# One tile and one write per block for the softmax weights p, loads without the own segment and partly from ScalarE's queue, q products a step later

## Chip, cores and metric

One core of a Trainium2 chip runs the whole program. The metric is the device time of one execution in microseconds (us). All arrays are float32; matmuls run in a float32 form for which every operand is split in two parts (below).

## What is computed

```python
xn = _layernorm(x)                        # x: 2048 x 512
q  = (xn @ wq)                            # 32 heads of 128
p  = softmax(q @ k.T * 128**-0.5)         # per head, the last 512 cached keys
o  = p @ v                                # per head, back to 128 columns
s  = concat(o) @ wo                       # 4096 -> 512
z  = gelu(xn @ w_in)                      # 688 + 688 columns
g  = w_sp @ layernorm(z[:, 688:]) + b_sp  # 2048 x 2048 times 2048 x 688
out = x + s * silu((z[:, :688] * g) @ w_out)
```

The first five lines are the attention part, to which the change belongs; it fills the span up to about 1535 us. The rest follows it.

## The kernel before, in words

**Two parts of every operand.** A value is kept as `hi` (rounded by ScalarE) and `lo` (the rest, from VectorE or GpSimd by `rest`, L59). A product is three matmuls, hi·hi, hi·lo and lo·hi (`mm3`, L65 to L67).

**Blocks and steps.** A block is one head with 512 rows of q; there are 128 blocks, and each has four steps of 128 rows, 512 steps `t` in all. One loop over `t` writes out the order of all engines by hand: each stage stands a fixed number of steps ahead of or behind the scores. In step `t`:

- `score(t)` (L468): q·k into a PSUM tile `ps_3` (ring of 4), the row maximum on VectorE (`nm`, L475), the exponential on ScalarE (`prob`, L477).
- `turn(t-1)` (L479): VectorE transposes the 32x32 squares of `prob` (L486) into a tile, SyncE (SP) writes that to HBM (`p_dram`, L491), and after a block's fourth step VectorE takes the reciprocal of the row sums (L493).
- `turned(b)` (L495), in step 4b+7: the turned p comes back from HBM into `pL` with the partition groups exchanged, so that keys stand on the partitions.
- `shares(b, c)` (L501), 11 steps after the score: ScalarE casts a quarter of p to `pT_h` (L506), GpSimd makes `pT_l`.
- `pv(b, c)` (L510), 13 steps after: p·v, summed in a PSUM tile `ps_a` (a pool of 4 banks); after the fourth one `pv_out` makes `oT_h` on ScalarE (L521) and `oT_l` on VectorE.
- `outp(b, j)` (L526), 18 steps after: o·wo into a `ps_3`, added to `sacc` on VectorE (L536).

**q.** From the second group of four blocks on, q is made by a scheme with seven products for two heads and two halves of the columns: `q_products` (L439 to L448) runs in the 16 steps that begin LEAD steps before the group's first score, `q_evict` (L451) and `q_done` take the results out. A group holds up to three `ps_a` banks; the one called `a` is read last by the eviction with index 6: `qT_h` on ScalarE (L378), then `qT_l` on VectorE. That `qT_l` is put on the list `late` and runs at a step's end, so the profile gives it the line of the loop over that list, L728.

**Queues.** Each engine works through its own instructions in order, SP and ScalarE their transfers too. Before, SP issues all transfers of the attention part: weights (`raw`, L102; `wq`, L409), p out and back, and stored parts of x (`rawx` to `x_dram`, L314; the fetches of L258 and L263). ScalarE issues only the stores of z1 (L358). Eight semaphores are shared by all transfers of both queues in turn, so a transfer can also wait for an earlier one that used its semaphore.

Of the kernel before, what the change touches and what calls it, by code (L numbers as in the profile page):

```python
# [8 lines left out]
F32 = mybir.dt.float32  # L9
# [8 lines left out]
P = 128  # L18
# [14 lines left out]

XL, QL, ML, PL, OL = 11, 7, 11, 13, 18
T8 = NT // 2
LEAD = 13
Q = 32


# [1 line left out]
def mixer_kernel(ctx: ExitStack, tc: tile.TileContext, x, wh, w_in, w_sp, b_sp, w_out, out):  # L41
# [8 lines left out]
    nc = tc.nc  # L50
# [3 lines left out]
    dram = ctx.enter_context(tc.tile_pool(name="dram", bufs=1, space=DRAM))  # L54
# [3 lines left out]
    def rest(engine, lo, whole, hi):  # L58
        engine.tensor_tensor(lo, whole, hi.bitcast(F32), op=OP.subtract)  # L59

    late = []
# [23 lines left out]
    att = ExitStack()  # L85
    sp = att.enter_context(tc.tile_pool(name="sp", bufs=1))
    ap = att.enter_context(tc.tile_pool(name="ap", bufs=2))
    wq = att.enter_context(tc.tile_pool(name="wq", bufs=2))
    zs = att.enter_context(tc.tile_pool(name="zs", bufs=2))
    xq = att.enter_context(tc.tile_pool(name="xq", bufs=4))  # L90
    sacc = sp.tile([P, T8, D], F32, name="sacc")


# [3 lines left out]
    raw, wt = {}, {}  # L97
# [5 lines left out]

    def load_early(n, cs):
        if (n, "raw") not in raw:
            raw[n, "raw"] = ap.tile([P, 16, P], F32, name="pL").rearrange("p k q -> p (k q)")
        for lo, hi in cs:
            nc.sync.dma_start(raw[n, "raw"][:, lo * NB:hi * NB].rearrange("p (c f) -> p c f", f=NB), w_in[n, :, lo:hi])
            for k in range(lo, hi):
                raw[("w", n), k] = raw[n, "raw"][:, k * NB:k * NB + NB]  # L110
# [237 lines left out]
    def z1_product(i, n, between=lambda: None):  # L348
        ps = ps_acc.tile([P, 512], F32, name="ps_a") if n else ps_step.tile([P, 512], F32, name="ps_3")
        zmm(ps[:, :NB], i, n, range(2))  # L350
        between()
        zmm(ps[:, :NB], i, n, range(2, NC))
        return ps
# [7 lines left out]
        z1_out(i, n, z1_product(i, n, between))  # L361


    pB = [None]
    qps, qT, pps, pD, pL, pT, oT, prob, sums = {}, {}, {}, {}, {}, {}, {}, {}, {}

    def where(b):
# [21 lines left out]
    def qproj(b, c):  # L389
        h, qb = where(b)  # L390
        if c == 0:
            qps[b] = ps_acc.tile([P, 512], F32, name="ps_a")
        mm3(qps[b], c == 0, c == NC - 1, cols(wt[("q", h), 0], c * P, (c + 1) * P),
            tuple(X[0][c // 2, qb][:, a, c % 2] for a in range(2)))
# [56 lines left out]
    def q_evict(g, k):  # L451
        ps = qps[g, BANK[k]]
        if k in (0, 2, 3):
            t = qps[g, "t", k] = ap.tile([P, 512], F32, name="qs", bufs=2)
            nc.scalar.activation(t, ps, AF.Copy, scale=SCALE)  # L455
        elif k in (1, 5):
            nc.vector.scalar_tensor_tensor(ps, ps, SCALE, qps[g, "t", {1: 0, 5: 2}[k]], op0=OP.mult, op1=OP.add)
        elif k == 4:
            t = qps[g, "t", 3]
            nc.vector.scalar_tensor_tensor(t, ps, SCALE, t, op0=OP.mult, op1=OP.add)  # L460
# [18 lines left out]
    def turn(t):  # L479

        b, j = divmod(t, 4)
        if j % 2 == 0:
            pB[0] = ap.tile([P, 4, 2, P], F32, name="pB", bufs=3)
        nc.vector.transpose(pB[0][:, :, j % 2, :].rearrange("p a (c q) -> p a c q", q=Q),  # L486
                            prob.pop(t).rearrange("p (a c q) -> p a c q", a=4, q=Q))
        if j == 0:
            pD[b] = dram.tile([2, P, 1024], F32, name="p_dram", bufs=3)
        if j % 2:  # L490
            nc.sync.dma_start(pD[b][j // 2], pB[0].rearrange("p a j f -> p (a j f)"))  # L491
        if j == 3:
            nc.vector.reciprocal(sums[b], sums[b])  # L493

    def turned(b):  # L495
        pL[b] = ap.tile([P, 8, 256], F32, name="pL")
        of = pD.pop(b).rearrange("s (i r) (a f) -> a r (s i) f", i=4, a=4)
        for a in range(4):
            nc.sync.dma_start(pL[b][Q * a:Q * a + Q], of[a])

    def shares(b, c):  # L501
        hi = ap.tile([P, 512], F32R, name="pT_h", bufs=4)
        lo = ap.tile([P, 512], F32R, name="pT_l", bufs=4)
        p = pL[b].rearrange("p i (j f) -> p (i j) f", j=2)[:, :, Q * c:Q * c + Q]
        h, l = (t.rearrange("p (i q) -> p i q", q=Q) for t in (hi, lo))
        nc.scalar.copy(h, p)  # L506
        rest(nc.vector if 4 * b + c >= NSTEP - 10 and c % 2 else nc.gpsimd, l, p, h)
        pT[b, c] = (hi, lo)
# [6 lines left out]
    def pv_out(b, c):  # L515
        if c == 3:
            hi = ap.tile([P, 512], F32R, name="oT_h")
            lo = ap.tile([P, 512], F32R, name="oT_l")
            ps = pps.pop(b).rearrange("p (s i j q) -> p s i j q", s=2, i=4, j=2)
            h, l = (t.rearrange("p (s j i q) -> p s i j q", s=2, i=4, j=2) for t in (hi, lo))  # L520
            nc.scalar.copy(h, ps)  # L521
            for k in range(2):
                late.append((rest, nc.vector, l[:, k], ps[:, k], h[:, k]))
            oT[b] = (hi, lo)

    def outp(b, j):  # L526
# [44 lines left out]
    for g in range(1, NG):  # L571
        t0 = 16 * g - LEAD
        loads.setdefault(max(T0, t0 - 12), []).append(g)
        sums_at, splits_at = (-5, -4, -2, 1), (-3, -1, 2, 4, 6, 7, 10)
        if g == 1:
            sums_at, splits_at = (-5, -4, 1, 3), (0, 1, 3, 5, 6, 8, 10)
        order = sorted([(s, 1, q_sum, k) for k, s in enumerate(sums_at)] + [(s, 0, q_split, k) for k, s in enumerate(splits_at)])
        for s, _, f, k in order:
            at(t0 + s, f, g, k)
        for k in range(7):  # L580
            done = next(s for s in range(16) if 6 * k + 5 in q_span(g, s))
            q_events.setdefault(t0 + done, []).append((q_evict, g, k))
            if k in (1, 4, 5):
                q_events.setdefault(t0 + done + 1, []).append((q_done, g, k))
            elif k == 6:
                q_events.setdefault(t0 + done + 2, []).append((q_done, g, k))
# [7 lines left out]
    for k, d in enumerate((4, 6, 8, 11, 13, 15, 17)):  # L594
        for n in range(4):
            ends.setdefault(16 * (NG // 2 - 1) - LEAD + d + (0, 0, 1, 1)[n], []).append((fetch_part, 1, ORDER[k], n))
    ends.setdefault(16 * (NG - 1) - LEAD + 9, []).append((fetch_x, 1, (0, 1)))
    for k in ((0, 0), (1, 0)):
        ends.setdefault(NSTEP + 6, []).append((fetch_x, 0, k))
    n = 0  # L600
    for p in range(4):
        seq, store = later_x(p)
        for f, ks in seq:
            t = 30 + 13 * n // 5
# [5 lines left out]

    load_x(0, 1)
    load_early(0, [(0, 2)])
    load_x(1, 2)
    load_early(0, [(2, 4)])
    load_x(2, 4)
    load_early(1, [(0, 4)])
    load_piece(("q", 0), 0)
    load_x(4, 8)
# [27 lines left out]
    ps = ps_step.tile([P, 512], F32, name="ps_3")  # L646
# [9 lines left out]
    ps = ps_step.tile([P, 512], F32, name="ps_3")  # L656
# [4 lines left out]
    ps = ps_acc.tile([P, 512], F32, name="ps_a")  # L661
# [18 lines left out]
    for t in range(T0, T1):  # L680
# [9 lines left out]
        i = t + XL  # L690
        if i < T8:
            ln_flip(i)
        if 0 <= bm < NBLK:
            shares(bm, cm)
# [8 lines left out]
        if 0 <= bq < 4:  # L703
            qproj(bq, cq)
        g, s = divmod(t + LEAD, 16)
        if 0 < g < NG:
# [5 lines left out]
        if t in DRAIN:  # L712
            ps = z1_product(*DRAIN[t])
# [19 lines left out]
    ps = z1_product(*LAST[-1])  # L733
# [276 lines left out]
```

## Time and profile before

| | us |
|---|---|
| median of 3 runs | 1907.47 |
| lowest, highest | 1906.44, 1908.14 |
| profiled execution, its own time | 1907.01 |
| span of its profile | 1905.1 |

PE is TensorE's matmul, PEld its weight load, DVE is VectorE, ACT ScalarE, POOL GpSimd; an SPq or ACTq row is an instruction in that queue. A row of waits reads: who waited, at which line, for whom, then us in total, times, and the longest. A row of a table by stages has the busy us of the five engines with their counts of instructions, the granted TensorE clock, the share of time in which the 16 DMA engines were busy, and what they moved in GB/s. A group of instructions shows its count, busy us in all, ns of one, and the idle us of its engine just before it with what ended them. In a timeline stand start, length, and in brackets the idle time before.

### The profile page before, as it was taken

The page shows a single profiled execution, that of the slowest core. Times are in us where ns is not written, and L with a number is a line of the kernel's source. Part 1 is how long each engine was busy: PE and PEld are TensorE (multiplying, and loading weights), DVE is VectorE, ACT ScalarE, POOL GpSimd, SP SyncE. Part 2 cuts the span into 40 slices and gives each one's busy share as a digit, 9 for nine tenths or more (in the row PEclk, how much of TensorE's full clock was granted, in tenths as well). Part 3 has the DMA queues.
Part 4 walks back from the last instruction along what each step waited for, and adds up shares of the span by engine and source line. Part 5 has one row for each costly group of instructions (what it writes and reads, how often), then busy time and mean ns, then how long its engine had stood idle before and what let it go on. Part 6 is the DMA issues. An engine that isn't in the chain of part 4 may idle for free.

```text
span 1905.1 us, 28198 instructions
## 1 busy us (share of the span) xinstructions
PE 1820.5 (96%) x8658; PEld 1540.4 (81%) x8658; DVE 1403.3 (74%) x2497; ACT 1179.1 (62%) x2631; POOL 1244.3 (65%) x1185
## 2 busy tenths in 40 slices
PE   8898999999999898999999999999999999999999
PEld 7776777777787686778887877878777899999998
DVE  5687888888888787788888888888888556333433
ACT  4666677777677575667677777777677545333422
POOL 3686798798798786788878888888888435000000
PEclk9998999999999999999999999999999999999999
DMA  5798999999999889999889899988999833545543
GB/s 180 198 282 228 237 264 242 251 265 239 252 264 244 216 248 296 267 270 247 236 239 241 241 241 245 245 237 245 236 246 260 257 134 119 194 146 168 158 134 96
DMA packets 277624, 429.16 MB, mean 225 GB/s; under 512 B 22272, under 2 KB 183808, under 8 KB 276320
## 3 DMA queue, kind: packets, MB, share of 16 engines
q1 hardware_dynamic: 272864, 421.72, 79.4%
q10 hardware_dynamic: 4608, 5.64, 0.8%
q8 instruction: 68, 1.11, 0.3%
q14 instruction: 84, 0.69, 0.1%
HBM read 260.55 MB, written 166.72 MB: 224 GB/s over the span
## 4 chain that ended last, share of the span: by engine, by line
PE 73%; DMA 11%; DVE 7%; ACT 3%; POOL 3%; issue 2%; SPq 1%; ACTq 0%; POOLq 0%; DVEq 0%
PE ps_a L448 11%; PE ps L65 9%; PE ps L67 9%; PE ps L66 9%; PE ps_a L65 7%; PE ps_a L66 6%; PE ps_a L67 6%; DMA pL<-p_dram 4%; PE ps_g L66 4%; PE ps_g L67 4%; PE ps_g L65 4%; DMA p_dram<-pB 2%; DVE sacc L536 2%; DVE pB L486 1%; ACT prob L477 1%
## 5 line engine op out<-in xcount | busy, mean ns | idle before, releaser
L59 POOL TENSOR_TENSOR pT_l<-pL,pT_h 128x512 fp32r<-128x512 f32 x507 | 657.9, 1298 | 265.5 <-ACT pT_h L506 250.7
L477 ACT ACTIVATE prob<-ps,nm 128x512 f32<-128x512 f32 x512 | 352.8, 689 | 290.9 <-DVE nm L475 285.1
L536 DVE SCALAR_TENSOR_TENSOR sacc<-ps,sums,sacc 128x512 f32<-128x512 f32 x496 | 369.6, 746 | 149.2 <-PE ps L67 144.2
L506 ACT CAST pT_h<-pL 128x512 fp32r<-128x512 f32 x512 | 318.1, 621 | 130.8 <-DMA pL<-p_dram 68.3
L448 PE MATMUL ps_a<-x,x 128*128 128x512 f32 x1302 | 378.6, 391 | 7.9 <-ACT qs L455 6.9
L486 DVE STREAM_TRANSPOSE pB<-prob 128x512 f32<-128x512 f32 x512 | 359.0, 701 | 23.2 <-ACT prob L477 22.4
L475 DVE TENSOR_REDUCE nm<-ps 128x1 f32<-128x512 f32 x512 | 338.8, 662 | 8.6 <-PE ps L67 8.5
L448 PEld LDWEIGHTS ps_a<-x,x 128*128 128x128 f32 x1302 | 245.9, 189 | 61.9 <-ACT qs L455 8.3
L59 POOL TENSOR_TENSOR wl<-raw,wh 128x512 fp32r<-128x512 f32 x192 | 249.2, 1298 | 9.0 <-ACT wh L141 9.0
L65 PE MATMUL ps_a<-pT_h,wh 128*128 128x512 f32 x512 | 204.2, 399 | 46.7 <-DVE qT_l L728 42.3
L65 PE MATMUL ps<-wh,qT_h 128*128 128x512 f32 x512 | 204.0, 399 | 8.6 <-DVE sacc L536 5.1
L66 PE MATMUL ps_a<-pT_l,wh 128*128 128x512 f32 x512 | 203.0, 396 | 7.3 <-POOL pT_l L59 7.1
L67 PE MATMUL ps_a<-pT_h,wl 128*128 128x512 f32 x512 | 200.9, 392 | 0.0
L66 PE MATMUL ps<-wl,qT_h 128*128 128x512 f32 x512 | 200.9, 392 | 0.0
L65 PE MATMUL ps<-wh,oT_h 128*128 128x512 f32 x512 | 200.7, 392 | 0.0
L66 PE MATMUL ps<-wl,oT_h 128*128 128x512 f32 x512 | 200.6, 392 | 0.0
L67 PE MATMUL ps<-wh,oT_l 128*128 128x512 f32 x512 | 200.6, 392 | 0.0
L67 PE MATMUL ps<-wh,qT_l 128*128 128x512 f32 x512 | 200.6, 392 | 0.0
L66 PE MATMUL ps_g<-z_l,x 128*128 128x344 f32 x512 | 162.1, 317 | 1.3 <-POOL z_l L59 1.3
L65 PE MATMUL ps_g<-z_h,x 128*128 128x344 f32 x512 | 162.1, 317 | 0.0
L67 PE MATMUL ps_g<-z_h,x 128*128 128x344 f32 x512 | 161.9, 316 | 0.0
L65 PEld LDWEIGHTS ps_a<-pT_h,wh 128*128 128x128 f32 x512 | 96.7, 189 | 79.2 <-DVE qT_l L728 55.0
(203 smaller groups left out, 3235.3 us busy)
## 6 DMA issues: line engine op xcount, KB each, us to landing
p_dram<-pB SPq DMA_DIRECT2D x256, 512.0 KB, 5.2
pL<-p_dram SPq DMA_DIRECT2D x512, 256.0 KB, 5.8
raw<-wh SPq DMA_DIRECT2D x194, 256.0 KB, 6.7
wq<-wh SPq DMA_DIRECT2D x62, 256.0 KB, 6.1
x<-w_sp SPq DMA_DIRECT2D x60, 256.0 KB, 6.0
x_dram<-rawx SPq DMA_DIRECT2D x32, 256.0 KB, 5.6
x<-x_dram SPq DMA_DIRECT2D x28, 256.0 KB, 7.6
u_dram<-uB SPq DMA_DIRECT2D x15, 384.0 KB, 2.3
```

The source lines that it names most:

```text
L59: engine.tensor_tensor(lo, whole, hi.bitcast(F32), op=OP.subtract)
L65: nc.tensor.matmul(ps, lh, rh, start=first, stop=False)
L66: nc.tensor.matmul(ps, lh, rl, start=False, stop=False)
L67: nc.tensor.matmul(ps, ll, rh, start=False, stop=last)
L448: nc.tensor.matmul(qps[g, bank], wt["q", g, k][a][:, c * P:(c + 1) * P], X[g * 2 // H][ORDER[k]][:, b, c], start=first, stop=r == 5, skip_ ...
L475: nc.vector.tensor_reduce(nm, ps, axis=AX.X, op=OP.max, negate=True)
L477: nc.scalar.activation(prob[t], ps, AF.Exp, bias=nm, accum_out=sums[b][:, j:j + 1])
L486: nc.vector.transpose(pB[0][:, :, j % 2, :].rearrange("p a (c q) -> p a c q", q=Q), prob.pop(t).rearrange("p (a c q) -> p a c q", a=4, q=Q))
L506: nc.scalar.copy(h, p)
L536: nc.vector.scalar_tensor_tensor(at, ps, rs, at, op0=OP.mult, op1=OP.add)
```

## The change

It turns a whole block of p in one tile `pL` (ring of 4), writes that in one transfer of 1 MiB after the fourth turn, and loads back into the same tile only the three quarters that come from other partition groups: a group's own segment stays where it is. Loads for partitions 64 to 127 are issued by ScalarE. In HBM the order of p is by source group, row, target group and column, so a piece is 512 elements long where it was 256. `pv_out` subtracts in one instruction and no longer two. LEAD goes from 13 to 12, which moves q's products, evictions and loads one step later. The rings of `rawx` and `qs` grow by one; the memory set aside for descriptors shrinks.

```diff
-LEAD = 13
+LEAD = 12
...
-    xq = att.enter_context(tc.tile_pool(name="xq", bufs=4))
+    xq = att.enter_context(tc.tile_pool(name="xq", bufs=5))
...
-            t = qps[g, "t", k] = ap.tile([P, 512], F32, name="qs", bufs=2)
+            t = qps[g, "t", k] = ap.tile([P, 512], F32, name="qs", bufs=3)
...
         b, j = divmod(t, 4)
-        if j % 2 == 0:
-            pB[0] = ap.tile([P, 4, 2, P], F32, name="pB", bufs=3)
-        nc.vector.transpose(pB[0][:, :, j % 2, :].rearrange("p a (c q) -> p a c q", q=Q),
+        if j == 0:
+            pL[b] = ap.tile([P, 4, 512], F32, name="pL", bufs=4)
+        nc.vector.transpose(pL[b][:, :, j * P:j * P + P].rearrange("p a (c q) -> p a c q", q=Q),
                             prob.pop(t).rearrange("p (a c q) -> p a c q", a=4, q=Q))
-        if j == 0:
-            pD[b] = dram.tile([2, P, 1024], F32, name="p_dram", bufs=3)
-        if j % 2:
-            nc.sync.dma_start(pD[b][j // 2], pB[0].rearrange("p a j f -> p (a j f)"))
         if j == 3:
+            pD[b] = dram.tile([4, Q, 4, 512], F32, name="p_dram", bufs=3)
+            nc.sync.dma_start(pD[b].rearrange("i r a f -> (i r) (a f)"), pL[b].rearrange("p a f -> p (a f)"))
             nc.vector.reciprocal(sums[b], sums[b])
 
     def turned(b):
-        pL[b] = ap.tile([P, 8, 256], F32, name="pL")
-        of = pD.pop(b).rearrange("s (i r) (a f) -> a r (s i) f", i=4, a=4)
+        of = pD.pop(b).rearrange("i r a f -> a r i f")
         for a in range(4):
-            nc.sync.dma_start(pL[b][Q * a:Q * a + Q], of[a])
+            for lo, hi in ((0, a), (a + 1, 4)):
+                if lo < hi:
+                    (nc.scalar if a > 1 else nc.sync).dma_start(pL[b][Q * a:Q * a + Q, lo:hi], of[a, :, lo:hi])
...
-            for k in range(2):
-                late.append((rest, nc.vector, l[:, k], ps[:, k], h[:, k]))
+            late.append((rest, nc.vector, l, ps, h))
...
-    nc = bacc.Bacc("TRN2", target_bir_lowering=False, num_devices=1)
+    nc = bacc.Bacc("TRN2", target_bir_lowering=False, num_devices=1, dynamic_dma_scratch_size=4096)
```

TensorE before, where a new group of four blocks begins its p·v, in step 16g+5. `ps_a_11741` is the q product's new bank of the step before it, `ps_a_11743` the p·v sum; `ps_3` are scores (with `qT`) and o·wo (with `oT`).

```order
L65 MATMUL ps_3_11732<-wh1_11421,qT_h_11615 128x512
L66 MATMUL ps_3_11732<-wl1_11422,qT_h_11615 128x512
L67 MATMUL ps_3_11732<-wh1_11421,qT_l_11616 128x512
L448 MATMUL ps_a_11665<-x8_8565,x8_737 128x512
L448 MATMUL ps_a_11741<-x8_8638,x8_737 128x512
L65 MATMUL ps_a_11743<-pT_h_11649,wh2_11491 128x512
L66 MATMUL ps_a_11743<-pT_l_11650,wh2_11491 128x512
L67 MATMUL ps_a_11743<-pT_h_11649,wl2_11492 128x512
```

The same place with the change, one step and a half of TensorE.

```order
L67 MATMUL ps_3_11563<-wh1_11263,qT_l_11480 128x512
L447 MATMUL ps_a_11537<-x8_8482,x8_751 128x512 x3
L65 MATMUL ps_a_11574<-pT_h_11484,wh2_11330 128x512
L66 MATMUL ps_a_11574<-pT_l_11485,wh2_11330 128x512
L67 MATMUL ps_a_11574<-pT_h_11484,wl2_11331 128x512
L65 MATMUL ps_3_11578<-wh3_11226,oT_h_11419 128x512
L66 MATMUL ps_3_11578<-wl3_11227,oT_h_11419 128x512
L67 MATMUL ps_3_11578<-wh3_11226,oT_l_11420 128x512
L65 MATMUL ps_3_11601<-wh1_11263,qT_h_11479 128x512
L66 MATMUL ps_3_11601<-wl1_11264,qT_h_11479 128x512
L67 MATMUL ps_3_11601<-wh1_11263,qT_l_11480 128x512
L447 MATMUL ps_a_11537<-x8_8482,x8_751 128x512
```

Before, the q product opened its second bank just ahead of the first p·v matmul of the group, in the same step; with the change the p·v sum opens its bank a step before the q product opens its second one (the next row after these). The matmuls are the same.

ScalarE's queue with the change, at the end of a step 4b+7, where before stood no transfer: a cast of p and the exponential of the step, the new loads of another block's p, then the next step's cast and exponential.

```order
L504 CAST pT_h_11355<-pL_11058 128x512
L476 ACTIVATE prob_11367,sums_11271<-ps_3_11361,nm_11365 128x512
L497 DMA pL_11191<-p_dram_11290 32x2x512
L497 DMA pL_11191<-p_dram_11290 32x512
L497 DMA pL_11191<-p_dram_11290 32x3x512
L504 CAST pT_h_11390<-pL_11058 128x512
L476 ACTIVATE prob_11402,sums_11399<-ps_3_11395,nm_11400 128x512
```

The three loads wait for the write of `p_dram_11290`, which SP issued three steps before; the cast and the exponential behind them wait with them.

SP's queue before, two writes and four loads per block, with the first write of the next block ahead of a block's loads:

```order
L491 DMA p_dram_12020<-pB_12018 128x1024
L499 DMA pL_12085<-p_dram_11891 32x8x256 x4
L102 DMA raw_12090<-wh 128x512
L491 DMA p_dram_12020<-pB_12083 128x1024
L491 DMA p_dram_12156<-pB_12154 128x1024
L499 DMA pL_12214<-p_dram_12020 32x8x256 x4
```

and with the change:

```order
L489 DMA p_dram_11290<-pL_11191 128x2048
L102 DMA raw_11294<-wh 128x512
L102 DMA raw_11324<-wh 128x512
L497 DMA pL_11191<-p_dram_11290 32x3x512
L497 DMA pL_11191<-p_dram_11290 32x512
L497 DMA pL_11191<-p_dram_11290 32x2x512
L102 DMA raw_11388<-wh 128x512
```

One write and three loads per block are left, and nothing of the next block stands between a block's write and its loads.

More of the change, by code (lines that the diff above doesn't have):

```diff
@@ L105, in load_early @@
         if (n, "raw") not in raw:
-            raw[n, "raw"] = ap.tile([P, 16, P], F32, name="pL").rearrange("p k q -> p (k q)")
+            raw[n, "raw"] = ap.tile([P, 16, P], F32, name="pL", bufs=4).rearrange("p k q -> p (k q)")
         for lo, hi in cs:
@@ L361, in z1_piece @@
         z1_out(i, n, z1_product(i, n, between))
-    pB = [None]
     qps, qT, pps, pD, pL, pT, oT, prob, sums = {}, {}, {}, {}, {}, {}, {}, {}, {}
@@ L503, in shares @@
         lo = ap.tile([P, 512], F32R, name="pT_l", bufs=4)
-        p = pL[b].rearrange("p i (j f) -> p (i j) f", j=2)[:, :, Q * c:Q * c + Q]
+        p = pL[b].rearrange("p i (j f) -> p (i j) f", j=4)[:, :, Q * c:Q * c + Q]
         h, l = (t.rearrange("p (i q) -> p i q", q=Q) for t in (hi, lo))
@@ L518, in pv_out @@
             lo = ap.tile([P, 512], F32R, name="oT_l")
-            ps = pps.pop(b).rearrange("p (s i j q) -> p s i j q", s=2, i=4, j=2)
-            h, l = (t.rearrange("p (s j i q) -> p s i j q", s=2, i=4, j=2) for t in (hi, lo))
+            ps = pps.pop(b).rearrange("p (i j q) -> p i j q", i=4, j=4)
+            h, l = (t.rearrange("p (j i q) -> p i j q", i=4, j=4) for t in (hi, lo))
             nc.scalar.copy(h, ps)
-            for k in range(2):
-                late.append((rest, nc.vector, l[:, k], ps[:, k], h[:, k]))
+            late.append((rest, nc.vector, l, ps, h))
             oT[b] = (hi, lo)
```

## The prediction

> **What bounds the kernel now.** I read the busy times first, then who waits for whom on TensorE (PE), then the busy times by stretches of 50 us, and last the timeline at the waits that come back.
>
> ```profile
> PE 1820.5 (96%) x8658; PEld 1540.4 (81%) x8658; DVE 1403.3 (74%) x2497; ACT 1179.1 (62%) x2631; POOL 1244.3 (65%) x1185
> PE ps_a L65 <- DVE qT_l L728: 42.3, 30, 7.8
> ```
>
> PE is busy for 1820.5 of 1905.1 us, so at most 84.6 us of idle time, and what a slower clock adds, can be won without removing a matmul. The second row is the largest wait of PE: half of that idle time, in 30 waits. L65 of `ps_a<-pT_h` is the first p·v matmul of a block: it needs a free `ps_a` bank, and the one it gets is freed by the last read of a q product, `qT_l` at L728 on VectorE (DVE). There are 31 q groups of four blocks, so this is one wait per group.
>
> ```profile
> PE ps_a L65 <- DVE qT_l L728: 3.9, 4, 1.0
> 942.08 0.70 DVE L486 STREAM_TRANSPOSE pB<-prob 128x512 f32<-128x512 f32 x1
> 942.76 0.66 DVE L728 SCALAR_TENSOR_TENSOR qT_l<-ps_a,qT_h 128x512 fp32r<-128x512 f32 x1
> 943.47 0.50 PE L65 MATMUL ps_a<-pT_h,wh 128*128 128x512 f32 x1 [0.97 <-DVE qT_l L728]
> ```
>
> The first of these rows is the same wait between 1000 and 1200 us only: 4 waits, 3.9 us, so about 0.97 us each where nothing else disturbs. The timeline shows why: `qT_l` stands on DVE behind the turn of a step that PE has already left, and PE's next step asks for the bank at once.
>
> ```profile
> 50.00:100.00 50.00, 45.19 (x199) 36.58 (x198) 32.37 (x55) 33.24 (x81) 33.29 (x37) 0.97 0.76 214
> 100.00:150.00 50.00, 45.06 (x195) 35.96 (x193) 38.39 (x68) 28.62 (x68) 35.36 (x33) 0.99 0.98 279
> 150.00:200.00 50.00, 45.03 (x190) 36.67 (x190) 40.00 (x74) 35.97 (x85) 41.20 (x41) 0.91 0.85 224
> 200.00:250.00 50.00, 44.44 (x193) 34.97 (x191) 40.44 (x75) 34.15 (x80) 39.11 (x38) 1.00 0.91 238
> 600.00:650.00 50.00, 42.30 (x176) 33.62 (x175) 36.23 (x68) 31.03 (x73) 34.87 (x34) 0.93 0.86 226
> 700.00:750.00 50.00, 46.78 (x196) 37.40 (x196) 39.85 (x71) 32.25 (x76) 38.99 (x38) 0.97 0.99 274
> 750.00:800.00 50.00, 41.59 (x168) 32.97 (x167) 32.97 (x59) 28.14 (x65) 31.78 (x30) 0.93 1.01 284
> 850.00:900.00 50.00, 47.13 (x201) 38.21 (x199) 40.69 (x73) 36.37 (x84) 41.67 (x38) 0.97 0.89 248
> 950.00:1000.00 50.00, 49.03 (x217) 40.29 (x216) 43.29 (x78) 34.77 (x82) 40.19 (x38) 1.00 0.89 240
> ```
>
> The columns are PE, PEld, DVE, ScalarE (ACT) and GpSimd (POOL), then the granted clock, the DMA share and GB/s. An undisturbed stretch (last row) takes 217 matmuls; I use 216. The eight rows above it lack 17, 21, 26, 23, 40, 20, 48 and 15: together 210, at 50/216 = 0.231 us each 48.6 us. Those are the second loss: 20 us between 50 and 250, 9.3 at 600, 15.7 between 700 and 800, 3.5 at 850. The count also takes in what a lowered clock costs.
>
> ```profile
> 640.58 0.41 ACT L309 CAST rawx<-rawx 128x256 fp32r<-128x256 f32 x1 [8.09 <-DMA x_dram<-rawx]
> 642.20 0.80 PE L448 MATMUL ps_a<-x,x 128*128 128x512 f32 x1 [6.29 <-ACT qs L455]
> 720.96 8.60 DMA p_dram<-pB
> 729.62 7.10 DMA pL<-p_dram
> 736.74 7.63 DMA x<-x_dram
> 744.39 10.00 DMA pL<-p_dram
> ```
>
> At 600 ScalarE stood 8.09 us because all four `rawx` buffers were still being stored, and PE behind it 6.29. At 700 to 800 the chain that ended last runs over DMA alone, p out and p back among it, with a DMA share of 0.99 and 1.01.
>
> **The change part by part.** The profiled execution took 1907.0 us (span 1905.1 and 1.9 around it), 0.5 below the median of 1907.47; I sum against 1907.0.
>
> *LEAD 12.* Every q product, its evictions and its loads move one step later against scores and p·v. In step 16g+5 the bank of `qT_l` (L728) is now not yet free, and the p·v matmul takes one freed two or more steps earlier; the q product that opens a bank in step 16g+6 takes one that `oT_l` freed two steps before. So the only PE wait for DVE over a single step in each group goes. What is late next is `sacc` and `oT_l`, two steps old. 30 x 0.97 = **-29 us**; the rest of the 42.3 (13 us) lies in the disturbed stretches and is counted there. Bounds: 0, if another wait ends just behind, and -42.3. The q results have one step less in hand; the tightest, the second block of a group, keeps two steps from eviction to score, as `sacc` has.
>
> *p in one tile, without the own segment, and five `rawx` buffers.* Per block of 128 p moves 1 MiB out in one DMA instead of two, and 0.75 MiB back in 2 KB pieces instead of 1 MiB in 1 KB pieces; beside it go 0.5 MiB of weights. 2.5 MiB per block become 2.25.
>
> ```profile
> DMA packets 61007, 96.64 MB, mean 242 GB/s; under 512 B 4700, under 2 KB 42174, under 8 KB 60974
> q1 hardware_dynamic: 60974, 96.26, 90.3%
> DMA packets 22770, 35.94 MB, mean 144 GB/s; under 512 B 2528, under 2 KB 9184, under 8 KB 22752
> q1 hardware_dynamic: 22752, 35.69, 44.6%
> ```
>
> The first two rows are 1000 to 1400 us, the others 1650 to 1900. 96.26 MB in 0.903 of 400 us are 267 GB/s at a full share, mostly small packets; 35.69 MB in 0.446 of 250 us are 320 with larger ones. 2.36 MB per block of 10.9 us then take a share of 0.81 by the first and 0.68 by the second, where it was 0.90. Stretches that stand at 1.0 fall by 10 to 25%, so transfers stop queueing. I credit the 9.3 us at 600 in full (the fifth buffer ends that wait) and six tenths of the other 39, since 10% less traffic alone would not clear them: **-33 us**. Bounds: 0, if latency and not load was the limit, and -49.
>
> *Three loads per block from ScalarE's queue.* New here is that ScalarE issues transfers, and that it waits for p's write before it may.
>
> ```profile
> L358 ACTq DMA_DIRECT2D z_dram<-z x32: 326/326/732, 12.6 to 1542.4; - x32
> L499 SPq DMA_DIRECT2D pL<-p_dram x512: 302/448/1700, 67.8 to 1514.8; - x171
> 1000.00:1043.65 43.65, 42.59 (x187) 34.62 (x186) 37.15 (x67) 30.99 (x72) 36.60 (x35) 1.00 0.91 241
> 932.64 0.14 DVE L493 RECIPROCAL sums<-sums 128x4 f32<-128x4 f32 x1
> 938.91 0.68 ACT L477 ACTIVATE prob<-ps,nm 128x512 f32<-128x512 f32 x1
> p_dram<-pB SPq DMA_DIRECT2D x256, 512.0 KB, 5.2
> x_dram<-x SPq DMA_DIRECT2D x4, 1024.0 KB, 8.0
> ```
>
> An issue takes 0.33 us (ScalarE's own row) to 0.45 (this shape, on SP): 1.0 to 1.3 us per block. In an undisturbed group of 43.65 us ScalarE is busy for 30.99, so each block leaves 3.2 us idle: the issue is hidden there, and would cost up to 128 x 1.3 = 170 us if that cover went. The wait: p's write can start when the fourth turn is done (the reciprocal follows it, 932.64), and ScalarE comes to its loads behind the exponential three steps on, which ends at 939.59, so some 6.9 us later. A write of 512 KB lands in 5.2 us, one of 1024 KB in 8.0; so the wait is 0 to 1.1 us per block. I take the row of the same size, 8.0. Behind the waiting instruction stand the next cast of p and the next exponential: GpSimd and then PE's p·v wait for the one, DVE's turn and a bank of `ps` for the other; PE asks for both two or more steps later, so most of 2.4 us is absorbed. I charge 0.3 us of PE per group, 32 groups: **+10 us**; bounds 0 and the slow rival below.
>
> The Trainium skill ("DMA: Bandwidth & Descriptors", Anatomy of one DMA) fits a transfer issued by GpSimd as 2.0 us plus its bytes over 436 GB/s, an estimate of 4.4 us for 1 MiB. By that ScalarE never waits, and the sum would be 1845 instead of 1855; the 8.0 us row, on a loaded core, speaks against it. The same page (Issuing engines are not separate DMA queues) holds that issuing from a second engine saves only the sequencer's issue time. By that the second queue buys nothing; I have credited nothing to it.
>
> *The rest.* `oT_l` in one piece saves DVE 0.1 us a block beside PE's work:
>
> ```profile
> L59 DVE TENSOR_TENSOR oT_l<-ps_a,oT_h 128x256 fp32r<-128x256 f32 x256 | 95.0, 412 | 50.3 <-ACT oT_h L521 50.2
> L59 DVE TENSOR_TENSOR qT_l<-ps_a,qT_h 128x512 fp32r<-128x512 f32 x62 | 42.9, 691 | 5.0 <-ACT qT_h L381 1.5
> ```
>
> Two of 412 ns against one of 691. I count nothing for it, nor for the third `qs`, the four `pL` tiles (the turn writes one whose last reader is three steps old), or SP, which issues four transfers per block and no longer six.
>
> Sum: 1907.0 - 29 - 33 + 10 = **1855 us**.
>
> **The rivals.** *The wait moves* (chance 0.25). ScalarE's burst of up to 2.4 us makes the casts of p late once per block, GpSimd passes it on, and PE waits 0.3 us per block instead of per group: 128 x 0.3 = 38 in place of 10 gives 1883. For it: ScalarE, DVE and POOL then all stand near 85% of a group. Against: the ring depth of two to three steps.
>
> *ScalarE becomes the bound, slower* (0.17). Per block it has 7.75 us of work and 1.2 of issue; with a wait over 1.95 us it passes the 10.9 us of a block. Arrival is 6.9 to 7.9 us after the write's start, so this begins where the 1 MiB write lands later than about 9.4 us, and outweighs the DMA gain from about 9.8. At 10.5 the wait is 3.15, the block 12.1; as arrival moves out by three quarters of the stretch, 1.2/1.75 = 0.69 us remain, 128 x 0.69 = 88, less 33: 1962 us. For it: even the 512 KB writes took up to 11.8 us at worst.
>
> ```profile
> DMA to landing us min/median/max: 2.6/5.2/11.8
> ```
>
> Against: that is the worst of 256, at the load that the change takes down.
>
> *It does not do what it says* (0.06): the bank taken is again a late one, and latency, not load, made the slow stretches: 1907.
>
> **How the numbers follow.** The forecast holds 0.52, by itself 1835 to 1880; the others 0.25, 0.17 and 0.06. Below 1835 lie the full bounds of both gains, 1907 - 42 - 49 + 0 = 1816, which need all to go well at once; the range starts at 1830. Its upper end, 1912, takes in the moved wait and no change, and leaves out the slow rival. 0.2% (3.8 us) is about what a measurement of this kernel can tell from no change. Faster: 0.52 + 0.25 = 0.77; same 0.05; slower 0.18.
>
> **What would show it.** Right: no wait of `ps_a` for `qT_l` of the scaled eviction; 43.65 us per group become 42.7; DMA share near 0.75 in undisturbed stretches; 700 to 800 above 205 matmuls per 50 us; ScalarE's loads waiting for `p_dram` under 1.5 us. Wrong: PE waiting for `pT_l`, `pT_h` or `prob` by tens of us; ScalarE over 90% busy or waiting; a 1 MiB write landing in 10 us or more; a share still at 0.9.

## The result and the profile after

| | before | after |
|---|---|---|
| median, us | 1906.95 (4 runs, 1903.32 to 1908.14) | 1857.06 (4 runs, 1851.29 to 1859.07) |
| ratio, 95% interval | | 0.9737 [0.9711, 0.9762] |
| profiled execution, us | 1907.01 | 1851.29 (span 1849.5) |

The change took 50 us (2.6%) off; the forecast was 1855. The sum agrees. Its three terms need a look of their own, since errors of opposite sign give the same sum. The views come in the order in which the prediction read them. First the busy times:

```profile
PE 1812.1 (98%) x8658; PEld 1538.9 (83%) x8658; DVE 1397.0 (76%) x2369; ACT 1181.6 (64%) x2631; POOL 1246.7 (67%) x1185
```

PE's idle time falls from 84.6 to 37.4 us (1849.5 - 1812.1), that is by 47; its busy time falls by 8.4 although no matmul went. Busy time can fall without any work going, for two reasons that these traces show. The granted clock was 0.991 on average before and is 0.995 now; worked out from these means (0.009 x 1905.1 less 0.005 x 1849.5), that alone is an estimate of 8 us. And a matmul that stands waiting counts partly as busy: two groups at a clock of 1.00, compared below under *LEAD 13 with all loads on SP*, differ by 0.24 us of busy time for the same work. Then who waits for whom on PE:

```profile
PE ps L65 <- DVE sacc L533: 12.1, 20, 1.9
PE ps_a L66 <- POOL pT_l L59: 6.3, 9, 0.9
PE ps_a L65 <- ACT pT_h L504: 2.1, 3, 1.2
```

The row of before with 42.3 us, the p·v matmul that waits for the late `qT_l`, is gone. As forecast, `sacc` comes next; but its 12.1 us in 20 waits are no wait of every group. Now the stretches of 50 us, the same as were shown of before, and an undisturbed one last:

```profile
50.00:100.00 50.00, 47.19 (x208) 37.71 (x207) 31.83 (x55) 33.48 (x83) 35.52 (x39) 0.97 0.61 196
100.00:150.00 50.00, 47.07 (x200) 36.73 (x199) 39.57 (x67) 33.08 (x78) 39.92 (x38) 1.00 0.86 271
150.00:200.00 50.00, 49.73 (x221) 40.62 (x220) 45.71 (x79) 38.91 (x90) 44.65 (x45) 1.00 0.77 224
200.00:250.00 50.00, 48.71 (x212) 38.98 (x212) 42.30 (x74) 35.18 (x86) 42.24 (x42) 1.00 0.81 244
600.00:650.00 50.00, 50.00 (x221) 41.10 (x220) 44.62 (x76) 37.97 (x91) 44.21 (x44) 1.00 0.82 248
700.00:750.00 50.00, 44.77 (x181) 34.05 (x179) 34.69 (x59) 28.87 (x69) 34.08 (x32) 0.97 0.89 285
750.00:800.00 50.00, 49.24 (x216) 40.20 (x215) 44.55 (x74) 37.06 (x87) 44.46 (x42) 1.00 0.83 249
850.00:900.00 50.00, 49.74 (x220) 40.81 (x219) 43.64 (x74) 36.70 (x85) 44.07 (x41) 1.00 0.75 216
950.00:1000.00 50.00, 50.00 (x222) 41.42 (x221) 44.91 (x76) 37.35 (x87) 42.42 (x41) 1.00 0.74 224
```

An undisturbed stretch now takes 222 matmuls, where it took 216, and PE has no idle time in it. The eight slow stretches of before lacked 210 matmuls (48.6 us); against 222 they lack 14, 22, 1, 10, 1, 41, 6 and 2, together 97, at 50/222 us each 21.8. Taken over all 27 stretches from 50 to 1400 us, the shortfall against the undisturbed rate was 59.7 us and is 35.4: beside these eight, four of the five stretches between 250 and 500, which lacked 3 to 6 before, now lack 6 to 10 each. One group, and p's transfers:

```profile
1000.00:1042.20 42.20, 42.20 (x188) 34.95 (x187) 37.40 (x64) 31.14 (x73) 36.79 (x35) 1.00 0.76 230
```
```profile
p_dram<-pL SPq DMA_DIRECT2D x128, 1024.0 KB, 4.7
```

A group takes 42.2 us where it took 43.65, and the forecast had 42.7. The DMA share went from 0.91 to 0.76. The 1 MiB write lands in 4.7 us, where the prediction had taken 8.0.

### The profile page after: what moved, and what is told of

Its sections match the earlier page's. It is cut to its first block, busy times and chain, and to the rows that moved or that the text cites. A ratio compares the mean times of both kernels' runs of the same rounds, so it can differ in the third digit from the quotient of the medians.

```text
span 1849.5 us, 28726 instructions
## 1 busy us (share of the span) xinstructions
PE 1812.1 (98%) x8658; PEld 1538.9 (83%) x8658; DVE 1397.0 (76%) x2369; ACT 1181.6 (64%) x2631; POOL 1246.7 (67%) x1185
## 4 chain that ended last, share of the span: by engine, by line
PE 79%; DMA 10%; DVE 4%; ACT 3%; POOL 2%; issue 2%; SPq 1%; ACTq 0%; DVEq 0%; POOLq 0%
PE ps_a L447 12%; PE ps L65 10%; PE ps L67 10%; PE ps L66 10%; PE ps_a L66 7%; PE ps_a L65 7%; PE ps_a L67 7%; PE ps_g L66 4%; PE ps_g L65 4%; PE ps_g L67 4%; DMA pL<-p_dram 4%; DMA p_dram<-pL 3%; DMA raw<-wh 1%; DVE nm L474 1%; ACT prob L476 1%
## 5 line engine op out<-in xcount | busy, mean ns | idle before, releaser
L504 ACT CAST pT_h<-pL 128x512 fp32r<-128x512 f32 x512 | 318.7, 622 | 181.3 <-DMA pL<-p_dram 41.8
L485 DVE STREAM_TRANSPOSE pL<-prob 128x512 f32<-128x512 f32 x512 | 358.9, 701 | 2.9 <-ACT prob L476 2.9
L59 DVE TENSOR_TENSOR oT_l<-ps_a,oT_h 128x512 fp32r<-128x512 f32 x128 | 88.2, 689 | 90.3 <-ACT oT_h L519 89.6
```

The costliest lines, as they stand in the source:

```text
L485: nc.vector.transpose(pL[b][:, :, j * P:j * P + P].rearrange("p a (c q) -> p a c q", q=Q), prob.pop(t).rearrange("p (a c q) -> p a c q", a ...
```

## Experiments

The theory on record: each term is about as in the sum (LEAD 29, transfers of p 33 together with the fifth `rawx` buffer, ScalarE's loads +10 through its wait for p's write). The rival: the gains are larger, and ScalarE's loads take back what is more, by their issue or by their wait. Each ratio is against the kernel before on the same chip (medians of before: 1903.08, 1906.43 and 1907.63 in the three sets); a difference of ratios is turned into us at 1907.

### LEAD alone

The kernel before with one line changed:

```diff
-LEAD = 13
+LEAD = 12
```

> The kernel before with LEAD 12 alone; p is stored and loaded as before. Theory (two separate losses): the bank wait for qT_l goes, the slow stretches stay: 1907 - 29 = 1878, an undisturbed group of 42.2 to 42.7 us, DMA share still 0.9 there. Rival (the order of q is the whole gain): 1857. Rival (p's transfers are the whole gain, the bank wait only followed from them): 1900 to 1907, and a new wait of PE in place of the old one.

Measured 1852.2 us (1849.42 to 1857.28), ratio 0.9728 [0.9698, 0.9758]: 52 us, as much as the whole change. The page and one group of this kernel:

```profile
PE 1807.2 (98%) x8658; PEld 1542.1 (83%) x8658; DVE 1405.0 (76%) x2497; ACT 1175.8 (64%) x2631; POOL 1245.4 (67%) x1185
```
```profile
1000.00:1042.20 42.20, 42.20 (x187) 34.93 (x187) 37.51 (x67) 31.00 (x74) 36.82 (x35) 1.00 0.94 250
```

The group takes 42.2 us here too, with a DMA share of 0.94. So the undisturbed group is LEAD's work alone, and a share of 0.94 costs such a group nothing. Its span is 1850.3 us, 54.8 less than before; 41.5 of them were PE's idle time and 13.3 its busy time. The slow stretches changed too, although p's path is the old one:

```profile
150.00:200.00 50.00, 50.00 (x220) 40.99 (x219) 46.72 (x85) 39.70 (x92) 46.42 (x47) 0.99 0.95 255
200.00:250.00 50.00, 48.47 (x212) 38.77 (x211) 43.09 (x80) 34.61 (x82) 41.95 (x41) 1.00 0.98 263
600.00:650.00 50.00, 44.37 (x187) 35.73 (x187) 38.78 (x72) 32.07 (x76) 37.94 (x37) 0.93 0.89 243
750.00:800.00 50.00, 46.70 (x204) 37.67 (x203) 40.29 (x71) 34.91 (x82) 40.01 (x38) 1.00 0.95 272
```

Before, they took 190, 193, 176 and 168 matmuls. From 50 to 1400 us the shortfall against the undisturbed rate is 40.8 us where it was 59.7. So about 19 us of LEAD's gain come from the slow stretches; the higher undisturbed rate is worth 36 over the same 1350 us (1350 x 6/222).

### LEAD back to 13 in the changed kernel

```diff
-LEAD = 12
+LEAD = 13
```

> The changed kernel with LEAD back at 13: only p's part and the rings are left. Theory (two separate losses): the 30 bank waits return, 1857 + 29 = 1886 to 1900, a group of 43.6 us, few slow stretches. Rival (order of q is the whole gain): 1907. Rival (p's transfers are the whole gain): 1857 to 1862.

Measured 1886.82 us, ratio 0.991 [0.9883, 0.9936]. Without LEAD the rest of the change brings 17 us. Since LEAD alone brings 52 and all together 50, the rest taken as a whole is worth 17 beside LEAD 13 and nothing that the times can tell beside LEAD 12.

### All loads on SP

```diff
-                    (nc.scalar if a > 1 else nc.sync).dma_start(pL[b][Q * a:Q * a + Q, lo:hi], of[a, :, lo:hi])
+                    nc.sync.dma_start(pL[b][Q * a:Q * a + Q, lo:hi], of[a, :, lo:hi])
```

> The changed kernel with all six loads of a block on SP. Theory (ScalarE pays a little for its three): 1845 to 1857, no more wait of ScalarE for p_dram, ScalarE with 1 us per block less to issue. Rival (the second queue is a gain of its own, loads land sooner by it): 1862 or more, with more waiting of the casts of p for pL than the 41.8 us of the changed kernel.

Measured **1825.18 us** (1823.97 to 1830.59), ratio 0.9588 [0.9563, 0.9612]. It beats both kernels, and neither case on record went below 1845. The second queue thus costs 0.0149, 28 us. Its span is 1828.8 us, and its page has:

```profile
PE 1797.6 (98%) x8658; PEld 1540.2 (84%) x8658; DVE 1395.2 (76%) x2369; ACT 1175.5 (64%) x2631; POOL 1244.2 (68%) x1185
```

The group that changes most is ScalarE's cast of p, in which the last field is the idle time of ScalarE just before these casts; first with all loads on SP, then the changed kernel:

```profile
L504 ACT CAST pT_h<-pL 128x512 fp32r<-128x512 f32 x512 | 318.4, 622 | 38.6 <-DMA pL<-p_dram 21.7 <-DMA wq<-wh 7.3 <-ACT z L357 3.2
```
```profile
L504 ACT CAST pT_h<-pL 128x512 fp32r<-128x512 f32 x512 | 318.7, 622 | 181.3 <-DMA pL<-p_dram 41.8 <-PE ps L67 41.6 <-PE ps_a L66 24.2
```

ScalarE stands 143 us more ahead of the casts. But it stands less ahead of the exponentials, again with all loads on SP first:

```profile
L476 ACT ACTIVATE prob<-ps,nm 128x512 f32<-128x512 f32 x512 | 354.0, 691 | 335.1 <-DVE nm L474 325.4
L476 ACT ACTIVATE prob<-ps,nm 128x512 f32<-128x512 f32 x512 | 352.9, 689 | 208.8 <-DVE nm L474 199.3
```

That is 126 us less, so most of the 143 came out of time in which ScalarE stood idle anyway. An undisturbed group takes 42.2 us here too:

```profile
1000.00:1042.20 42.20, 42.20 (x188) 34.95 (x187) 37.19 (x63) 30.96 (x72) 36.78 (x35) 1.00 0.75 226
```

So the cost lies elsewhere: over the stretches from 50 to 1400 us the shortfall is 21.8 us here and 35.4 in the changed kernel. These 13.6 us are two thirds of the 20.7 by which the two profiles differ; the rest lies outside these stretches.

### All loads on ScalarE

```diff
-                    (nc.scalar if a > 1 else nc.sync).dma_start(pL[b][Q * a:Q * a + Q, lo:hi], of[a, :, lo:hi])
+                    nc.scalar.dma_start(pL[b][Q * a:Q * a + Q, lo:hi], of[a, :, lo:hi])
```

> The changed kernel with all six loads of a block on ScalarE's queue. Theory (issue time on ScalarE is real but hidden): six issues are 2.3 us of a block's 3.2 idle, time within 1857 to 1867. Rival (issue runs beside ScalarE's arithmetic and costs nothing): 1857 within 3. Rival (hidden room is used up): 1880 or more, PE waiting for pT_l and prob.

Measured 1994.91 us, ratio 1.0458 [1.0441, 1.0476].

```profile
L504 ACT CAST pT_h<-pL 128x512 fp32r<-128x512 f32 x512 | 318.4, 622 | 355.3 <-PE ps L67 86.7 <-DMA pL<-p_dram 81.1 <-PE ps_a L447 48.8
```

Three loads cost 28 us, six cost 166 (1.0458 - 0.9588): the idle time before the casts only doubles, the price rises sixfold. That fits a ScalarE whose spare time covers the first issues and not the later ones, and the third case on record (1880 or more), though PE waits most for `oT_l` and `sacc` (36.6 and 34.0 us) and not, as that case has it, for `pT_l` and `prob`. But p also comes back later here, since ScalarE reaches its first load 3.1 us after the write has landed (median), and the two were not separated.

### One load on ScalarE

```diff
-                    (nc.scalar if a > 1 else nc.sync).dma_start(pL[b][Q * a:Q * a + Q, lo:hi], of[a, :, lo:hi])
+                    (nc.scalar if a > 2 else nc.sync).dma_start(pL[b][Q * a:Q * a + Q, lo:hi], of[a, :, lo:hi])
```

> The changed kernel with one load of p per block on ScalarE (partitions 96 to 127) and five on SP. Zero, three and six loads there gave ratios of 0.9588, 0.9737 and 1.0458, so 32 us for three and 170 for six. If each issue has the same price up to three: 1836, ratio 0.964 to 0.966. If idle time of ScalarE covers the first ones and only the rest costs: 1823 to 1830, ratio 0.957 to 0.961. If any wait of ScalarE for p's write costs, however few loads follow: near 1850, ratio 0.971.

Measured 1834.04 us, ratio 0.9611 [0.9595, 0.9628]: 4 us over none at all, with intervals that overlap. Since one load has to wait for p's write just as three have, a wait that costs at the first load is ruled out.

### Issues without p

All loads of p on SP, and in the same place three small transfers on ScalarE that nothing reads and that wait for nothing of p. They are added work, not part of the computation.

```diff
+        for k in range(3):
+            d = ap.tile([Q, 2, 8], F32, name="idle", bufs=6)
+            nc.scalar.dma_start(d, wh[k, 0:2 * Q, 0, 0:8].rearrange("(i r) f -> r i f", i=2))
```

> The changed kernel with all six loads of p on SP (1825.2 us, 0.9588 of the kernel before), and in the same place of the step three transfers on ScalarE that nobody reads: 32 x 16 values of a weight into a tile of its own, 4 KB each, waiting for nothing of p. p is complete as early as with all loads on SP; only ScalarE's queue has its three issues back. Theory A, the issues themselves hold ScalarE up (302 to 355 ns each in the quiet, up to 1.6 us where the DMA queues are full): the 32 us come back for the most part, 1845 to 1860, ratio 0.968 to 0.976. Theory B, the upper quarters of p come late because ScalarE reaches its loads only behind other work, and the issues cost nothing: 1823 to 1830, ratio 0.957 to 0.961, and ScalarE's cast of p waits about as little before it (38.6 us in all) as with all loads on SP.

Measured 1871.4 us, ratio 0.9805 [0.9786, 0.9823]: 41 us over all loads on SP, more than the three real loads cost, and above the range of either theory. The instructions and the casts behind them (three lines further down in this kernel):

```profile
L500 ACTq DMA_DIRECT2D idle<-wh x384: 317/451/1877, 66.9 to 1472.9; - x192
```
```profile
L507 ACT CAST pT_h<-pL 128x512 fp32r<-128x512 f32 x512 | 318.3, 622 | 192.7 <-DMA pL<-p_dram 64.0 <-PE ps L67 22.5 <-PE ps_a L67 20.7
```

The idle time before the casts is there again (192.7 us). But the run does not single out the issue, as it was meant to, because SP suffered too:

```profile
SPq L497 <- DMA idle<-wh: 169.2, 70, 5.9
SPq L489 <- DVE sums L490: 19.2, 2, 18.1
```

SP's loads of p stood 169.2 us for the added transfers. The wait for the next block's turn, which shows how much time SP has to spare, fell to 19.2 us; it is 206.9 with all loads on SP. p's write went out 3.6 us after the reciprocal behind the fourth turn (median), where with all loads on SP it went out at once, and the casts waited 64.0 us for p's loads where it was 21.7. So p was not complete as early as the expectation assumes, and the rival, p late, is not excluded. How much of the 41 us is the issues' own is open.

### The loads one and two steps earlier

Both undo the slack between p's write and the loads. An earlier step puts ScalarE's loads in front of the landing.

```diff
-        if t % 4 == 3 and 0 <= t // 4 - 1 < NBLK:
+        if t % 4 == 2 and 0 <= t // 4 - 1 < NBLK:
```

> The changed kernel with p's loads one step earlier in every queue, so that ScalarE comes to them some 4.2 us after the write began and no longer 6.9; the write takes 4.7 us. Theory (a wait of under 2 us per block is hidden on ScalarE): waits of ScalarE's queue for p_dram of about 0.5 us per block, time within 1857 plus or minus 5. Rival (any wait in ScalarE's queue goes through to PE): 128 x 0.5 = 64 us more, 1920.

> The changed kernel with p's loads two steps earlier, so that ScalarE comes to them some 1.5 us after the write began. Theory (the slow rival of the prediction, forced): a wait of 3.2 us per block, with 7.75 of work and 1.2 of issue 12.15 against 10.55 for a block; as arrival moves out by a quarter of the stretch, 1.6/1.25 = 1.28 us remain, 128 x 1.28 = 164: about 2020 us, ScalarE busy or waiting all the time. Rival (issue costs nothing in the engine's own time, so only the wait counts): 7.75 + 3.2 = 10.95, 0.3 us per block, about 1900.

One step earlier (the diff): 1856.21 us, ratio 0.9731 [0.971, 0.9753], no different from the changed kernel. Two steps earlier (`t % 4 == 1`): 1976.1 us, 1.0359 [1.0335, 1.0382]. The stops of ScalarE before a cast that the profile calls "issue", in the first and in the second, and one such stop of the second:

```profile
ACT pT_h L504 <- issue: 60.9, 32, 9.7
```
```profile
ACT pT_h L504 <- issue: 302.3, 98, 6.3
1013.58 1.32 ACTq L497 DMA_DIRECT2D pL<-p_dram  x3
1014.93 0.62 ACT L504 CAST pT_h<-pL 128x512 fp32r<-128x512 f32 x1 [2.49 <-issue]
```

Such a stop holds both the wait for p's write and the issues: of the 2.49 us shown, 1.32 are three issues. 32 stops of 1.9 us cost nothing; 98 of 3.1 cost 119 us over the changed kernel. A block of 10.55 us leaves 2.8 beside ScalarE's 7.75 us of work, so a stop of 3.1 is more than it has and one of 1.9 is not. The mechanism of the slow rival fits this; SP's loads moved too, and what they cost was not separated. Its price was only roughly met: its own stretch cost 88 us (1962 + 33 - 1907), the expectation of this run had 164 over the changed kernel, and the measured 119 lies between. In the changed kernel the write landed far too early to set it off (8.1 us at the latest).

### Four `rawx` buffers

```diff
-    xq = att.enter_context(tc.tile_pool(name="xq", bufs=5))
+    xq = att.enter_context(tc.tile_pool(name="xq", bufs=4))
```

> The changed kernel with four rawx buffers again. Theory (the fifth ended the 8 us stop of ScalarE near 600 us): one to four waits of ScalarE for x_dram come back, 1857 + 3 to 9. Rival (with less DMA traffic the stores land early enough): 1857 within 3, no such wait.

Measured 1856.94 us, ratio 0.9751 [0.9722, 0.978]: not to be told from the changed kernel. Its wait and its stretch at 600:

```profile
ACT rawx L309 <- DMA x_dram<-rawx: 12.3, 4, 5.2
```
```profile
600.00:650.00 50.00, 48.65 (x214) 39.39 (x213) 43.88 (x76) 37.33 (x88) 42.72 (x42) 1.00 0.81 244
```

The stretch takes 214 matmuls with four buffers and 221 with five; before, it was 176, and with LEAD alone 187. The fifth buffer ends a wait and saves some 1.6 us there (7 x 50/222), which is below what the times can tell; the faster transfers did the rest of it.

### LEAD 13 with all loads on SP

All loads on SP, as above, and:

```diff
-LEAD = 12
+LEAD = 13
```

> The changed kernel with all six loads on SP and LEAD back at 13: p's new layout and transfers without LEAD and without ScalarE's loads. If LEAD is worth what it was alone (ratio 0.9728, 51 us): 1825 + 51 = 1876, ratio 0.984 to 0.987. If it is worth what it took away beside the loads on ScalarE (1886.8 - 1857 = 30 us): 1855, ratio 0.973 to 0.976. The prediction credited the transfers with 33 us, so by it 1874.

Measured 1866.81 us, ratio 0.9784 [0.977, 0.9799]: p's new path without ScalarE brings 41 us beside LEAD 13, and 0.9728 - 0.9588 = 27 us beside LEAD 12. LEAD brings 52 us alone and 37 beside the new path. The ratio lies between the cases on record. Together the two changes bring 79 and not 93, so some 14 us could be won by either. The slow stretches show which: their shortfall from 50 to 1400 us is 59.7 before, 40.8 with LEAD alone, 23.8 with p's path alone and 21.8 with both. One group and the wait of this kernel:

```profile
1000.00:1043.40 43.40, 42.44 (x187) 34.82 (x186) 37.08 (x63) 31.12 (x73) 36.82 (x35) 1.00 0.74 219
```
```profile
PE ps_a L65 <- DVE qT_l L725: 37.7, 30, 6.3
```

Against 42.20 us the group is 1.20 longer: 0.96 of idle PE and 0.24 of PE that counts as busy. 31 groups by 1.20 are the 37 us.

### The own segment loaded too

```diff
-            for lo, hi in ((0, a), (a + 1, 4)):
+            for lo, hi in ((0, 4),):
```

First in the changed kernel (two of the four loads are ScalarE's), then with all four on SP.

> The changed kernel, but each of the four loads of a block brings all four segments, its own one too: 1 MiB back as before, in 2 KB pieces, four loads and no longer six (two on SP, two on ScalarE). Theory (bytes cost): DMA share in undisturbed stretches up from 0.76 to about 0.83, 1857 + 2 to 8, in the slow stretches. Rival (the piece size, not the bytes, is what took DMA down): within 3 us of 1857, or faster by the two issues that go.

> The changed kernel with all loads on SP and the own segment loaded too: four loads per block, of 256 KB each, in place of six, and 33 MB more in all. If neither bytes nor SP's issue time bind: as with six loads on SP, 1823 to 1831, ratio 0.957 to 0.962. If fewer issues on SP bring p back earlier: 1815 to 1822, ratio under 0.957. If the bytes count once the queue is not held up by ScalarE: 1832 to 1840, ratio 0.963 to 0.967.

In the changed kernel: 1851.54 us, ratio 0.9712 [0.9688, 0.9737], no worse than without. On SP alone: 1887.72 us, 0.9904 [0.9879, 0.9929], 60 us over the six loads on SP, and none of the three cases on record gave that. The first run by itself would have said that the saved segment is worth nothing; it also took one of ScalarE's three issues away, and the two may cancel; they were not separated. SP's waits with the own segment, then without it:

```profile
SPq L497 <- DMA p_dram<-pL: 828.3, 126, 9.3
SPq L489 <- DVE sums L490: 27.2, 7, 18.0
```
```profile
SPq L497 <- DMA p_dram<-pL: 431.5, 119, 6.9
SPq L489 <- DVE sums L490: 206.9, 99, 17.7
```

Without it SP has time left: 99 times it waits for the next block's turn. With it SP waits for its own writes. From its queue late in the attention part, other rows left out, with start and length:

```profile
1008.08 0.43 SPq L489 DMA_DIRECT2D p_dram<-pL  x1
1016.39 1.74 SPq L497 DMA_DIRECT2D pL<-p_dram  x4
1018.23 0.38 SPq L489 DMA_DIRECT2D p_dram<-pL  x1
1026.31 1.75 SPq L497 DMA_DIRECT2D pL<-p_dram  x4
1051.37 0.43 SPq L489 DMA_DIRECT2D p_dram<-pL  x1
```

From the first write to the last of these are four rounds in 43.29 us, 10.82 each, where a block has 10.55 (42.2/4): the write goes out behind the four loads, lands some 8 us later, and the next loads, which stand behind it in SP's queue, wait for it. The medians of p's write in the two kernels, with the own segment and without:

```profile
p_dram<-pL SPq DMA_DIRECT2D x128, 1024.0 KB, 8.4
```
```profile
p_dram<-pL SPq DMA_DIRECT2D x128, 1024.0 KB, 4.9
```

So what the saved segment buys, with one queue, is that SP's round of write, landing and loads ends before the next block. This is read from the two traces; no run changed the round by itself, and why the write needs 8 us even where it goes out later is open.

## Why the prediction held, step by step

Its total was right and its three terms were not. The gains are 17 us larger than 62, ScalarE's cost is 18 us larger than 10, and the two errors cancel. That the total came out so close is luck.

| term | forecast | measured |
|---|---|---|
| LEAD 12 | -29 (0 to -42.3) | -52 alone, -37 beside the new path of p |
| p in one tile, own segment, fifth buffer | -33 (0 to -49) | -41 alone, -27 beside LEAD 12 |
| both | -62 | -79 |
| three loads on ScalarE | +10 | +28 (+24 beside LEAD 13) |
| sum | -52 | -50 |

*LEAD 12.* The mechanism was right: the one wait of each group that hangs on a single step goes, and nothing as long stands behind it. The size failed at "30 x 0.97". The row of the wait on PE counts idle time only. The same wait on the weight loads' own row, in the profile of before, was longer:

```profile
PEld ps_a L65 <- DVE qT_l L728: 55.0, 30, 8.3
```

The group's period says what it is worth: LEAD alone took it from 43.65 to 42.20, by 1.45 us, and beside p's new path from 43.40 to 42.20. The bound of 42.3 was the idle row's sum, and LEAD alone passed it: to the period's gain came about 19 us in the slow stretches, which the prediction had given to p's transfers alone.

*p's transfers.* -33 lies between -27 and -41. What the DMA does between 1000 and 1400 us, first in the changed kernel, then with the own segment on SP:

```profile
q1 hardware_dynamic: 25777, 75.44, 61.5%
q10 hardware_dynamic: 9120, 14.95, 14.8%
```
```profile
q1 hardware_dynamic: 36912, 96.31, 82.1%
```

The share of 0.763 lies between the two estimates of 0.81 and 0.68. The second row moves as much as the kernel before (96.26 MB at 90.3%), in pieces of 2 KB for p: the larger pieces took 8 points, and the bytes left out the next 6. The reason given for the gain was only half right. "Stretches that stand at 1.0 fall, so transfers stop queueing" held for one of the three stretches that had stood near 1.0: 750 to 800 went from 168 to 216 matmuls, but 100 to 150 only from 195 to 200, and 700 to 750 from 196 to 181, against "above 205" on the list. Of the other stretches that recovered, at 150, 200 and 600 with shares of 0.85 to 0.91, the first two do so with LEAD alone as well (220 and 212 matmuls), and of the step from 168 to 216 at 750 LEAD alone makes 36. Only the recovery at 600, from 187 with LEAD alone to 221, is mainly the transfers' own. And the 9.3 us "in full" for the fifth buffer belonged to the faster transfers.

*ScalarE's loads.* Here the step failed that says "each block leaves 3.2 us idle: the issue is hidden there". All of the 10 us stood for the wait, and the issue stood at nothing; the runs showed that the loads cost 28 us with next to no wait. The write lands in 4.7 us at the median and ScalarE's first load starts 6.6 us after its issue (median of the 128 blocks, 5.7 at least); in 13 blocks it starts within 0.2 us of the landing. Even the stops of 1.9 us, one step earlier, cost nothing. What is left is the loads themselves:

```profile
L497 ACTq DMA_DIRECT2D pL<-p_dram x384: 309/355/1642, 69.0 to 1455.3; - x192
```

In an undisturbed group they are indeed hidden (42.2 us with and without). One block there shows how:

```profile
1008.45 0.69 ACT L476 ACTIVATE prob<-ps,nm 128x512 f32<-128x512 f32 x1 [0.53 <-DVE nm L474]
1008.50 0.79 ACTq L497 DMA_DIRECT2D pL<-p_dram  x2
1009.32 0.43 ACTq L497 DMA_DIRECT2D pL<-p_dram  x1
1009.86 0.62 ACT L504 CAST pT_h<-pL 128x512 fp32r<-128x512 f32 x1 [0.63 <-PE ps L67]
```

Two of the three issues run beside the exponential, and only 0.63 us stand open before the cast. (The row names a matmul for that gap; the issue lies in it.) Over the whole run 84 of the 154 us of these issues lie beside ScalarE's arithmetic. The price is paid elsewhere: 200 to 250 takes 212 matmuls against 224 with all loads on SP, 50 to 100 takes 208 against 219. Neither a busier ScalarE nor a long issue marks these places: ScalarE is busy for 35.18 of 50 us at 200 to 250 and for 37.35 at 950 to 1000, where nothing is lost and where the longest issue, 1.64 us, falls.

How the 28 us come about is therefore open. Two ways fit. ScalarE's own time is one. For it speaks that the same loads cost 24 us beside LEAD 13 (0.991 - 0.9784), where the casts waited 20.4 us for p's loads against 14.8 with all on SP, so that p was hardly later there. A later p is the other: in the changed kernel the casts waited 41.8 us for p's loads against 21.7, and SP's writes of p stood 52.0 us for earlier loads of p against 1.6. From the casts to PE neither was followed: PE's own row for `pT_h` has 2.1 us, and of the 20.7 us between the profiles (1849.5 and 1828.8) 14.5 are time in which PE counts as busy (1812.1 and 1797.6), in part by the granted clock (0.995 and 0.998).

A price like this was in the prediction, under *the wait moves*: 38 us in place of 10. For this term that rival came nearer than the forecast, but not by its mechanism: it has ScalarE late for the wait and PE late in every block, and the undisturbed groups lose nothing.

The Trainium skill ("DMA: Bandwidth & Descriptors", Anatomy of one DMA) gave an estimate of 4.4 us for a 1 MiB transfer; the trace has 4.7 for SP's write, so its fit, made for GpSimd's transfers, was nearer than the row of 8.0 that spoke against it. The sum of 1845 that followed from it was still no better, because the 10 us were not the wait. The same page (Issuing engines are not separate DMA queues) says that a second issuing engine saves only issue time. In the change the second one lost 28 us. With the own segment loaded too it won 37 (0.9904 on SP alone, 0.9712 with two of the four loads on ScalarE). That is 0.29 us per block, within the 0.9 us of issue time that it took off SP (two of four issues of 1.75 us together); whether it was that time was not separated.

*The rest.* Nothing was counted for the shorter `oT_l`, for `qs` or for SP. No run separates the first two. SP was not neutral: the saved segment is what keeps SP's round inside a block once it has all the loads.

## What to carry to other kernels

Transfers issued by an engine that stands in the chain of a stage can cost time although that engine has idle time in every block: here one load per block cost about 4 us, three 28 and six 166. Keep them on an idle queue where one is free, and try one alone before moving three. Look at what an added probe does to the other queues before reading its time: here it took SP's spare time away. Size a stall by the period of the loop it sits in, not by the idle row of the waiting engine. When a change has several parts, run the largest alone and leave the most doubtful out: here one line was worth the whole gain, and one more line gave back 28 us of it.

## What the runs showed of the hardware that was not expected

- With the same bytes in 400 us (96.3 MB), the new layout, with p read in 2 KB pieces, took a DMA share of 0.821 where the old one with 1 KB pieces took 0.903; yet a group took 42.2 us at a share of 0.94 as well as at 0.76.
- A 1 MiB write landed in 4.7 to 4.9 us (medians) in the changed kernel and with all its loads on SP. With 1 MiB of loads per block it took 6.5 us where these were on two queues and 8.4 where they were on SP's alone; the 512 KB writes of before took 5.2.
- One issue on ScalarE took 309 to 1642 ns, median 355. In the changed kernel 84 of the 154 us that 384 issues took ran beside ScalarE's own arithmetic; two steps earlier, where ScalarE had to wait for p's write first, 1 of 172 did.
- A transfer in one engine's queue can hold another queue: SP's loads of p stood 169.2 us for 384 small transfers of ScalarE that move nothing of p.
